# A gated linear attention and a cosine MoE layer on one core: more chunks loaded as pairs of tokens, the first ones by halves of the heads, and a new order

## The chip, the cores and the metric

The kernel runs on one core of one Trainium2 chip. The metric is the device time of one execution in microseconds (us). 13 runs of the kernel before gave a median of 196.63 us, from 194.6 to 198.44.

## What is computed

```python
# q, k, v, f_logit: (4, 8, 768, 48) float32
f = 1.0 / (1.0 + np.exp(-f_logit))
for t in range(S):
    state = f[:, :, t, :, None] * state + np.einsum('bhd,bhe->bhde', k[:, :, t], v[:, :, t])
    y[:, :, t] = np.einsum('bhd,bhde->bhe', q[:, :, t], state)
x = y.transpose(0, 2, 1, 3).reshape(3072, 384)
h = x @ w_in            # (3072, 2048)
g = h * np.cos(h)
out = g @ w_out         # (3072, 384)
```

## The kernel before

**Attention in chunks.** The 768 steps of each of the four batches are cut into six chunks of 128, 24 chunks in all, numbered 0 to 23. `decay` treats two neighbouring chunks at once: it loads f, takes exp and ln on ACT (ScalarE), sums the logarithms along the chunk with matmuls (`cum`, into PSUM), and makes the two factors `b` and `bi` with two more exps (`eb`, `ei`). `attend` then works on one chunk. It scales q and k (`qk`, on POOL), casts v (`vb`, `vz`), turns q and k so that the head dimension lies on the partitions (`tr` on PE and a copy `qkt`, or one DMA transpose `tq` for the chunks in `TURN_QK`), makes the scores (`sc`) and masks them (`am`, on DVE), makes the chunk's own share of the state (`ps`) and moves the state on (`st`, `sz`), and makes the result (`y`) directly in the transposed form that the MoE layer reads (`xe` copies it to `xT`).

**Pairs of tokens.** Chunks whose number is in `DUAL` are handled by `attend2`, two chunks at once. There a partition holds two neighbouring tokens, so that a row of a load is 384 bytes long, where that of a single chunk has 192. One load brings 384 KB for both chunks. The matmuls then work on tiles of 64 x 64 and 64 x 128, and the result is not transposed: `finish` casts it (`yb`), turns it on PE (`trx`) and copies it to `xT`. Before, `DUAL` is [0, 2, 4].

**The MoE layer.** `moe` takes units of 128, 128 and then 256 tokens. For each tile of 1024 columns in PSUM there are the w_in matmuls (`h`), a cosine on ACT (`cos`, the sine table with a shift of half pi) and a product on DVE (`g`, into `gT`). The w_out matmuls (`o`) sum 16 parts for each 128 tokens, in four pieces of four; the sum is copied (`ot`) and stored. The eight weight loads go through the `gT` buffers and are cast to bf16 (`wc`).

**What sets the order.** All operations are first collected in a `Plan` with their readers and writers. `Plan.run` (line 157) is a list scheduler: each operation has a cost for each engine that may do it, and a priority from the table `PR`; among those that can start within `WINDOW` of the earliest, the one of the lowest priority is put next on its engine. `PIN` fixes the engine for single operations. The result is a fixed order of instructions for each of the five engines. The costs only shape this order; the chip runs it as its data comes. All loads, stores and DMA transposes are issued by SP, in one queue. ACT needs two function tables, one for exp and ln and one for the sine; `gate` names for each group of four chunks the cosine that must come before its exps. There are six groups, and ten table loads. In the trace nearly all instructions carry line 257, which is the helper that records them; they are told apart by their tiles.

The SP queue of before begins with f, k, q (chunks 0 and 1), f (2 and 3), the first w_in, v (0, 1), k and q (2, 3), the second w_in, v (2, 3), k (4, 5) and the two remaining w_in. DMAs use eight semaphores in turn, so that each waits for the one eight places before it.

Of the kernel before, what the change touches and what calls it, by code (L numbers as in the profile page):

```python
# [111 lines left out]
class Op:  # L112
    __slots__ = ("seq", "eng", "fn", "prio", "table", "deps", "vals", "alloc", "start", "end",
                 "lat", "waiting", "after", "grp", "dma", "name", "prior", "cost", "made")


class Plan:
# [3 lines left out]
    PE_LAT = 180.0  # L121
    TABLE = 1290.0
    WINDOW = 30.0
# [4 lines left out]
    def op(self, name, eng, fn, reads=(), writes=(), prio=0.0, table=None, lat=0.0, grp=None,  # L128
           dma=None):
        o = Op()  # L130
# [3 lines left out]
        o.lat, o.grp, o.dma, o.prior = lat, grp, dma, []  # L134
# [22 lines left out]
    def run(self):  # L157
        free = {"PE": 0.0, "ACT": 800.0, "DVE": 3500.0, "POOL": 4500.0, "SP": 750.0}
        table, lock, bus, hot, pe_end = None, None, 0.0, 0.0, 0.0
# [9 lines left out]
        while len(order) < n:  # L169
            cand = []  # L170
            for o in ready:
# [18 lines left out]
                for e, cost in o.eng.items():  # L190
                    if e == "ACT" and lock is not None and o.grp != lock and o.table is not None:
                        continue
                    s = max(at, free[e] + (self.TABLE if e == "ACT" and o.table not in (None, table) else 0.0))
                    if pick is None or s + cost < pick[0]:
                        pick = (s + cost, s, e, cost)
# [19 lines left out]
            if e == "PE":  # L215
                hot *= math.exp((pe_end - s) / 2500.0)
                if hot < 0.5:
                    cost *= 1.9
                hot = 1.0 - (1.0 - hot) * math.exp(-cost / 2500.0)
                pe_end = s + cost  # L220
            o.start = s
            free[e] = s + cost
            if o.dma is not None:
                bus = max(s + cost + 700.0, bus) + o.dma
                o.end = bus + 1250.0
            else:
                o.end = s + cost + (self.PE_LAT if e == "PE" else 55.0 if e in ("ACT", "DVE") else 0.0)
                o.lat = o.end - s - cost
# [16 lines left out]


class Recorder:


    def __init__(self, engine, to):  # L250
        self._engine, self._to = engine, to

    def __getattr__(self, name):
        f = getattr(self._engine, name)

        def call(*a, **k):
            r = f(*a, **k)  # L257
            self._to.append(r.ins)
            return r
        return call  # L260


class Recorded:


    def __init__(self, nc):
        self.made = []
        for e in ("tensor", "vector", "scalar", "gpsimd", "sync"):
            setattr(self, e, Recorder(getattr(nc, e), self.made))


def apart(tc, o, base):
# [13 lines left out]
    if banks and len(others) == len(banks):  # L286
        for b in banks:
# [6 lines left out]
DUAL = [0, 2, 4]  # L294
FREE_GROUPS = 1
TURN_QK = range(12, 23)
PR = {
    "at": [-1.49, -6.93, -0.99, 13.27, -7.67, 4, 10, 9.5, -13.37, -12.55, -11.45, -9.46, -5.68, -7.15, -2,
          22.25, 10.19, 29.34, 19.9, 34.5, 43, 12.41, -1.95, 31.38],
    "dec": [-16.49, -13.88, -91.65, -10.62, -83.82, -35.17],  # L300
    "f": [-9.6, 0.04, -7, 14.37, 5.77, 13.7, 13.23, 18.93, 28.46, 33.49, 42.79, 22.57, 32.28, 13.8, 48.59,
          29.13, 41.13, 37.7, 30.11, 39.36, 49.42, 43.32, 46.86, 29.8],
    "h": [11.93, 4.6, -12.58, 7.32, -8.64, -9.43, 45, 2.23, 18.23, 18.63, 15.73, 4.41, 40.33],
    "k": [-7.62, -12.49, 0.44, 4.43, 2.7, -4.14, 7.69, 8.97, 12.29, 13.88, 14.32, 13.45, 12.51, 16.1, 9.18,
          19.51, 19.9, 19.74, 16.52, 18.13, 30.05, 34.16, 29.67, 47.94],
    "o": [14.78, 2.53, 13.63, 59.13, 65.36, 91.49, 25.09, 54.02, 36.97, 50.99, 62.96, 92.68, 123.05],
    "tq": [-17.43, -2.03, 6.77, 12.87, 14.04, 0.67, 25.22, 16.03, 47.81, 44.2, 43.57, 57.2, 54.62, 18.84,
          32.62, 19.95, 19.22, 16.34, 30.78, 4.33, 28.86, 63.13, 50.35, 20.78],
    "v": [-1.12, 8.51, 2.65, 15.87, 8.53, -6.56, 7.91, 9.09, 9.69, 12.52, 8.72, 6.57, 17.65, 13.3, 20.76,
          15.97, 19.8, 22.21, 13, 24.77, 21.05, 40.77, 28.44, 22.56],  # L310
    "w_in": [-3.97, 0.54, 2.78, 2.77],
    "w_out": [14.63, 52.89, 69.53, 73.7],
    "wc": [20.5, -34.04, -32.41, -65.79, -1.36, -30.8, -15, -24.5],
    "gate": [None, 8, 12, 14, 12, 32],
}
PIN = {1: "ACT", 9: "DVE", 11: "POOL", 13: "DVE", 28: "POOL", 29: "POOL", 32: "ACT", 46: "DVE", 48: "ACT", 51:
       "ACT", 64: "ACT", 92: "POOL", 93: "POOL", 94: "DVE", 96: "ACT", 111: "DVE", 113: "ACT", 116: "DVE", 158:
       "POOL", 161: "ACT", 173: "ACT", 176: "ACT", 178: "DVE", 220: "POOL", 223: "ACT", 237: "ACT", 239: "DVE",
       247: "ACT", 268: "DVE", 274: "ACT", 289: "POOL", 290: "POOL", 307: "ACT", 309: "ACT", 338: "DVE", 359:
       "ACT", 360: "POOL", 370: "ACT", 376: "POOL", 377: "ACT", 404: "ACT", 410: "DVE", 425: "ACT", 426: "POOL",  # L320
       434: "DVE", 440: "POOL", 441: "POOL", 450: "DVE", 471: "DVE", 477: "ACT", 492: "POOL", 508: "POOL", 509:
       "ACT", 539: "ACT", 560: "POOL", 561: "ACT", 570: "DVE", 576: "POOL", 577: "ACT", 624: "POOL", 633: "ACT",
       639: "POOL", 640: "POOL", 670: "DVE", 676: "DVE", 692: "ACT", 701: "DVE", 707: "POOL", 708: "ACT", 738:
       "DVE", 759: "ACT", 775: "ACT", 776: "ACT", 778: "DVE", 782: "ACT", 803: "ACT", 809: "ACT"}


def build(nc, cpool, ppool, q, k, v, f_logit, moe_w_in, moe_w_out, out, rec=None):
# [85 lines left out]
    P, nc = Plan(), rec or nc  # L413
# [17 lines left out]
    def load_weights(part, i, prio):  # L431
# [12 lines left out]
        P.op(f"w{part}{i}", {"SP": 420.0}, fn, writes=[stage], prio=prio, dma=2080.0)  # L444
# [7 lines left out]
    def load(t, src, b, c, n, prio, nm, eng="SP"):  # L452

        def fn(e):
            i_, o = (nc.scalar if e == "ACT" else nc.sync), t.ap
            if n not in DUAL:
                i_.dma_start(out=HB(o), in_=src[b, :, c * C:(c + 1) * C, :].rearrange("h p d -> p h d"))
            else:
                i_.dma_start(out=o.rearrange("p (h x) -> p h x", h=H),
                             in_=src[b, :, c * C:(c + 2) * C, :].rearrange("h (p e) d -> p h (e d)", e=2))  # L460
        P.op(nm + str(n), {eng: 430.0 if n not in DUAL else 500.0}, fn, writes=[t], prio=prio,
             dma=1000.0 if n not in DUAL else 1430.0)

# [11 lines left out]
    def decay(chunks, g, prio):  # L475
# [3 lines left out]
        pc = Val(scS if m == 2 else p1S)  # L479
        flat = lambda a: a.rearrange("p m h d -> p (m h d)")  # L480
        for i, (b, c, n) in enumerate(chunks[:1] if dual else chunks):
            load(ft.part((lambda a: flat(a)) if dual else (lambda a, i=i: a[:, i].rearrange("p h d -> p (h d)"))),
                 f_logit, b, c, n, PR["f"][n], "f")

        first = P.op("exp", {"ACT": act(384 * m, "S")}, lambda e: nc.scalar.activation(
            out=flat(ft.ap[:, 0:m]), in_=flat(ft.ap[:, 0:m]), func=AF.Exp, scale=-1.0),
            reads=[ft], writes=[ft], prio=prio, table="E", grp=g)
        gates.append((first, g))
        firsts.setdefault(g, []).append(first)
        loads = [w for p in ft.parts for w in p.writers]  # L490
# [3 lines left out]

        def ln(e):
            o, i_ = sp.ap[:, 0:m, :, 0:D], ft.ap[:, 0:m]
            if dual:
                o = o.rearrange("p e h d -> p h e d")
                i_ = i_.rearrange("p m h d -> p (m h) d").rearrange("p (h e) d -> p h e d", e=2)
            nc.scalar.activation(out=o, in_=i_, func=AF.Ln, bias=1.0)  # L500
        P.op("ln", {"ACT": act(384 * m, "S")}, ln, reads=[ft], writes=[sp], prio=prio, table="E", grp=g)
        cut = (lambda i: pc.ap[:, 512 * i:512 * i + 512]) if m == 2 else (lambda i: pc.ap)
        two = lambda j, h: sp.ap[:, j, h:h + 2, :].rearrange("p h d -> p (h d)")

        for i in range(m):
            def pe(e, i=i):
                o = cut(i)
                if dual:
                    w = sp.ap[:, :, 4 * i:4 * i + 4, 0:D]
                    v = o[:, 0:HD].rearrange("p (h e d) -> p h e d", e=2, d=D)  # L510
                    nc.tensor.matmul(v, lhsT=incl, start=True, stop=False,
                                     rhs=w[:, 0, :, None, :].broadcast_to([128, NP, 2, D]))
                    nc.tensor.matmul(v[:, :, 0, :], lhsT=strict, rhs=w[:, 1], start=False, stop=False)
                    nc.tensor.matmul(v[:, :, 1, :], lhsT=incl, rhs=w[:, 1], start=False, stop=False)
                    for p in range(2):
                        for x in range(2):
                            nc.tensor.matmul(o[:, HD + p:HD + NP:2], lhsT=two(x, 4 * i + 2 * p), rhs=half,
# [383 lines left out]
```

## Time and profile before

| | |
|---|---|
| median of 13 runs | 196.63 us (194.6 to 198.44) |
| the profiled execution | 194.6 us |
| its span from the first to the last instruction | 192.8 us |
| mean granted TensorE clock | 0.982 |
| busy: PE matmul / weight load | 173.8 us (90%) / 128.2 us (67%) |
| busy: DVE / ACT / POOL | 122.9 us (64%) / 129.3 us (67%) / 75.4 us (39%) |
| DMA queue of SP | 106240 packets, 32.78 MB, 78.3% of 16 engines |
| chain that ended last, by engine | PE 55%, DMA 19%, SP's queue 7%, ACT 6%, DVE 5% |

The span is counted from the first to the last instruction; 1.8 us of the profiled execution's time lie around it. A row of the timeline gives the start in us from the beginning of the span, the duration in us, the engine, the operation, the tile written and the tiles read with their shapes, how often in a row, and in brackets how long the engine had been idle before and what ended that. PE's matmuls overlap, so a block's cost is read from its start to the start of the next block, not from its duration. A matmul row such as `48*128` gives the part of the array in use, and then the shape of the operands. In the row of slices each digit is the busy share of 1/40 of the span in tenths; PEclk is the granted clock.

### The profile page before, as it was taken

What the parts mean: (1) busy time and instruction counts of PE and PEld (TensorE: products, weight loads), DVE (VectorE), ACT (ScalarE), POOL (GpSimd) and SP (SyncE); (2) the same over time, 40 slices, a digit from 0 to 9 for tenths busy, and PEclk for the clock granted to TensorE, in tenths of its full rate; (3) what the DMA queues carried; (4) which work ended last, traced back from release to release, by engine and by line L of the source; (5) the groups of instructions that cost most, each with busy time, mean ns of one, the idle gap of its engine ahead of it and who ended that gap; (6) DMA issues with size and microseconds to landing.
All of it is one profiled execution on the core that took longest, in us unless ns stands there. A gap on an engine that the chain in (4) does not pass through costs nothing.

```text
span 192.8 us, 5285 instructions
## 1 busy us (share of the span) xinstructions
PE 173.8 (90%) x2194; PEld 128.2 (67%) x2194; DVE 122.9 (64%) x152; ACT 129.3 (67%) x163; POOL 75.4 (39%) x119
## 2 busy tenths in 40 slices
PE   0385799999999998799999999999999999999992
PEld 0264699866688855567775668876667767787661
DVE  5147779947887571568697368895388576578200
ACT  3694768987868599595869966788866552476010
POOL 8337322309931215939761696212960420000000
PEclk9999589999999999999999999999999999999999
DMA  6999999999899888999999999999232301100222
GB/s 153 295 281 316 359 247 320 177 253 306 166 180 198 187 191 204 200 213 179 211 177 210 137 238 190 220 154 250 87 81 57 86 14 41 44 0 15 77 75 82
DMA packets 106264, 33.11 MB, mean 172 GB/s; under 512 B 99584, under 2 KB 104704, under 8 KB 106240
## 3 DMA queue, kind: packets, MB, share of 16 engines
q1 hardware_dynamic: 106240, 32.78, 78.3%
q8 instruction: 17, 0.28, 0.6%
q14 instruction: 7, 0.06, 0.1%
HBM read 25.17 MB, written 4.72 MB: 155 GB/s over the span
## 4 chain that ended last, share of the span: by engine, by line
PE 55%; DMA 19%; SPq 7%; ACT 6%; DVE 5%; issue 4%; POOL 3%; ACTq 0%; DVEq 0%; POOLq 0%
PE ps L257 55%; DMA ld<-in_v_dram 9%; SPq L257 7%; DMA gT<-in_moe_w_out_dram 4%; DMA qkt<-qk 3%; ACT cosh L257 3%; POOL qk L257 2%; DMA ld<-in_q_dram 2%; DMA f<-in_f_logit_dram 2%; DVE am L257 2%; ACT f L257 1%; DVE w_out_bf L257 1%; ACT L865 1%; DVE gT L257 1%; ACT xT L257 0%
## 5 line engine op out<-in xcount | busy, mean ns | idle before, releaser
L257 DVE TENSOR_TENSOR gT<-ps,cosh 128x1024 bf16<-128x1024 f32 x48 | 58.0, 1220 | 18.3 <-ACT cosh L257 16.3
L257 PE MATMUL ps<-xT,w_in_bf 128*128 128x256 bf16 (+1 forms) x624 | 68.5, 267 | 0.7 <-ACT xT L257 0.4
L257 PE MATMUL ps<-w_out_bf,gT 128*128 128x384 bf16 x384 | 68.3, 326 | 0.4 <-DVE w_out_bf L257 0.4
L257 ACT ACTIVATE cosh<-ps,halfpi 128x1024 bf16<-128x1024 f32 x48 | 53.0, 1113 | 23.2 <-PE ps L257 22.9
L257 PEld LDWEIGHTS <-w_in_bf 128*128 128x128 bf16 x624 | 57.2, 99 | 8.9 <-DVE xT L257 0.5
L257 PEld LDWEIGHTS <-gT 128*128 128x128 bf16 x384 | 35.3, 98 | 22.9 <-issue 0.5
L257 POOL TENSOR_TENSOR qk<-ld,b 128x384 bf16<-128x384 f32 x22 | 23.3, 1067 | 22.3 <-ACT b L257 9.7
L257 POOL TENSOR_TENSOR sz<-st,b 64x192 bf16<-64x192 f32 x32 | 16.1, 502 | 24.7 <-DVE st L257 23.1
L257 DVE TENSOR_TENSOR am<-ps,umask 128x1024 bf16<-128x1024 f32 x18 | 21.9, 1219 | 5.2 <-PE ps L257 5.1
L257 POOL TENSOR_TENSOR qk<-ld,bi 128x384 bf16<-128x384 f32 x22 | 22.6, 1037 | 0.2
L257 POOL CAST vb<-ld 128x384 bf16<-128x384 f32 x13 | 6.6, 505 | 28.8 <-DMA ld<-in_v_dram 22.3
L257 PEld LDWEIGHTS <-qk 128*128 128x128 bf16 (+1 forms) x212 | 12.5, 107 | 6.6 <-issue 2.4
L257 ACT COPY ot<-ps 128x384 f32<-128x384 f32 x14 | 6.7, 489 | 13.8 <-PE ps L257 13.7
L257 PE MATMUL ps<-ident,qk 128*128 128x128 bf16 x104 | 9.4, 240 | 4.0 <-DVE qk L257 2.2
L257 ACT ACTIVATE f<-f 128x768 f32<-128x768 f32 x12 | 9.7, 840 | 4.9 <-DMA f<-in_f_logit_dram 4.9
L257 ACT ACTIVATE b<-ps 128x776 f32<-128x776 f32 x12 | 9.9, 823 | 3.7 <-PE ps L257 2.7
L257 DVE TENSOR_TENSOR st<-ps,sz 128x384 f32<-128x384 f32 x16 | 8.8, 551 | 5.4 <-PE ps L257 4.1
L257 PEld LDWEIGHTS <-qkt 48*128 48x128 bf16 (+2 forms) x260 | 7.2, 107 | 6.8 <-issue 2.6
L257 PE MATMUL ps<-qkt 48*128 48x128 bf16 (+1 forms) x240 | 9.9, 234 | 1.8 <-ACT qkt L257 1.6
L257 DVE COPY ot<-ps 128x384 f32<-128x384 f32 x10 | 5.5, 554 | 8.7 <-PE ps L257 4.7
L257 ACT ACTIVATE bi<-ps 128x768 f32<-128x768 f32 x12 | 9.8, 818 | 0.0
L257 PE MATMUL ps<-sp,incl 128*128 128x384 bf16 (+1 forms) x12 | 4.0, 379 | 6.3 <-ACT sp L257 6.3
(64 smaller groups left out, 158.0 us busy)
## 6 DMA issues: line engine op xcount, KB each, us to landing
f<-in_f_logit_dram SPq DMA_DIRECT2D x18, 192.0 KB, 3.9
ld<-in_v_dram SPq DMA_DIRECT2D x18, 192.0 KB, 4.8
ld<-in_k_dram SPq DMA_DIRECT2D x18, 192.0 KB, 3.9
ld<-in_q_dram SPq DMA_DIRECT2D x18, 192.0 KB, 4.0
out_dram<-ot SPq DMA_DIRECT2D x18, 192.0 KB, 1.9
gT<-in_moe_w_in_dram SPq DMA_DIRECT2D x4, 768.0 KB, 7.5
gT<-in_moe_w_out_dram SPq DMA_DIRECT2D x4, 768.0 KB, 7.4
f<-in_f_logit_dram SPq DMA_DIRECT2D x3, 384.0 KB, 6.0
```

Source lines behind the costliest of these rows:

```text
L257: r = f(*a, **k)
L865: nc.scalar.preload_act_table_set("natural_log_exp_and_others")
```

## The change

- **Pairs.** `DUAL` becomes [0, 2, 4, 6, 8, 10, 12]: chunks 0 to 13, fourteen in all, are loaded and computed as pairs of tokens, where it was 0 to 5.
- **Halves.** For the pairs in `HALVED`, [0, 2], which are the first four chunks, f, k and q are each loaded by two DMAs of four heads. `decay` there runs exp, ln, cum, eb and ei once for each half of the heads, each depending only on its half, and `attend2` multiplies each half when its parts are there. v is not halved.
- **Turns.** `TURN_QK` becomes 16 to 22: q and k of chunks 12 to 15, which a DMA had turned, are turned on PE.
- **The last store.** The w_out matmuls of the last 128 tokens are made and stored in two pieces of 256 and 128 columns.
- **The order.** The planner gets new constants, a price for changes of the matmul tile form, and a limit on the loads in flight; `PR` and `PIN` have new values throughout (left out below). The engines' orders differ from beginning to end. The SP queue now begins with f by halves for chunks 0 and 2, then k, q, k, q by halves and v of chunk 0, the same of chunk 2, and then the four w_in, the first w_out, f and v of chunk 4, the second w_out, f of chunk 6, k and q of chunk 4 and the last two w_out. ACT casts no w_in any more: POOL and DVE cast two each. Of the w_out parts POOL casts three and DVE one.
- **Recording.** The instructions that an operation makes are collected by a callback of the builder, where a wrapper around the engines did it. The rule by which waits are set is the same.

Counted by instructions: of the multiplications `qk` DVE has 10 where it had 4, and POOL 38 where it had 44. PE has 140 matmuls more, POOL and SP have fewer instructions.

```diff
-DUAL = [0, 2, 4]
+DUAL = [0, 2, 4, 6, 8, 10, 12]
 FREE_GROUPS = 1
-TURN_QK = range(12, 23)
+HALVED = [0, 2]
+TURN_QK = range(16, 23)
...
-    "gate": [None, 8, 12, 14, 12, 32],
+    "gate": [None, 2, 5, 12, 18, 34],
...
-    PE_LAT = 180.0
+    PE_LAT = 150.0
+    FORM = 96.0
     TABLE = 1290.0
-    WINDOW = 30.0
+    WINDOW = 120.0
...
+                    if e == "PE" and o.form[0] != form:
+                        s = max(at, free[e] + self.FORM)
...
                 bus = max(s + cost + 700.0, bus) + o.dma
                 o.end = bus + 1250.0
+                sent.append(bus)
+                if len(sent) > 3:
+                    free[e] = max(free[e], sent[-4] + 900.0)
...
+    def load(t, src, b, c, n, prio, nm, flat=lambda a: a):
+
+        if n not in DUAL:
+            P.op(nm + str(n), {"SP": 430.0}, lambda e: nc.sync.dma_start(
+                out=HB(t.ap), in_=src[b, :, c * C:(c + 1) * C, :].rearrange("h p d -> p h d")),
+                writes=[t], prio=prio, dma=1050.0)
+            return
+        m = 2 if n in HALVED and nm != "v" else 1
+        for i in range(m):
+            w = H // m
+            dst = t.part(lambda a, i=i: flat(a)[:, i * HD:(i + 1) * HD]) if m == 2 else t
+            P.op(nm + str(n), {"SP": 470.0}, lambda e, i=i, w=w, dst=dst: nc.sync.dma_start(
+                out=(dst.ap if m == 2 else flat(dst.ap)).rearrange("p (h x) -> p h x", h=w), in_=src[
+                    b, w * i:w * i + w, c * C:(c + 2) * C, :].rearrange("h (p e) d -> p h (e d)", e=2)),
+                writes=[dst], prio=prio + 0.01 * i, dma=1500.0 / m)
...
+        halved = chunks[0][2] in HALVED
+        two = lambda j, h: sp.ap[:, j, h:h + 2, :].rearrange("p h d -> p (h d)")
+        for part in ([0], [1]) if halved else (list(range(m)),):
+            s, w = slice(part[0], part[-1] + 1), len(part)
+            of = lambda v, i=part[0]: v.parts[i] if halved else v
+            if halved:
+                for v in (sp, bt, bi):
+                    v.part(lambda a: a)
+            prio += 0.001 * part[0]
+            first = P.op("exp", {"ACT": act(384 * w, "S")}, lambda e, s=s: nc.scalar.activation(
+                out=flat(ft.ap[:, s]), in_=flat(ft.ap[:, s]), func=AF.Exp, scale=-1.0),
+                reads=[of(ft)], writes=[of(ft)], prio=prio, table="E", grp=g)
...
-                    reads=[src, dec], writes=[parts[j][i]], prio=prio)
+                    reads=[v.parts[i] if v.parts else v for v in (src, dec)], writes=[parts[j][i]], prio=prio)
...
+            pieces = [(0, d_model)] if r0 + C < n_tokens else [(0, 256), (256, d_model)]
+            for a, z in pieces:
+                po, half = Val(p1S), ot.part(lambda o, a=a, z=z: o[:, a:z]) if len(pieces) > 1 else ot
+                for s in range(4):
+                    def g2(e, i=i, s=s, po=po, a=a, z=z):
+                        for j in range(4 * s, 4 * s + 4):
+                            nc.tensor.matmul(po.ap[:, 0:z - a], lhsT=gT.ap[:, j, i * C:(i + 1) * C],
+                                             rhs=w_out_bf[:, j, a:z], start=(j == 0), stop=(j == KF - 1))
```

## The prediction, as it was put on record

> **What bounds the kernel now.** I read the page first (busy times and the 40 slices), then the table of waits, then the timeline of the first 48 us, and last the timeline of PE alone, from which I take a price for each block of matmuls.
>
> ```profile
> PE   0385799999999998799999999999999999999992
> ...
> PEclk9999589999999999999999999999999999999999
> DMA  6999999999899888999999999999232301100222
> ```
>
> Each character is 4.8 us. PE is nearly full from the fifth slice to the end: 173.8 us busy of a span of 192.8. What it lacks lies in the first four slices, in a dip at 72 to 95 us, and behind the last matmul. DMA is full for 28 slices (135 us), so early and middle stages can wait for loads although PE is the bound overall. PE's own waits name the places: 8.3 us for the first decay results (6.3 of it the very first), then in the timeline 0.41 us at 47.7 (a w_out cast whose DMA came at 46.0), 0.76 at 72.8, 1.19 at 81.2, 0.30, 0.18 and 0.35 up to 94.7. That is 3.2 us in the middle. The 1.19 us comes behind an exp that waited 2.31 us for an f load; the 0.76 comes behind a vz cast that waited 1.74 us for a v load, which delayed the cosines and with them the table load and the exp. The middle gaps are late loads. The end: the last matmul issues until 189.4, one copy of 0.48 us, one store, 192.8.
>
> The start is a race of loads:
>
> ```profile
> 11.11 1.47 ACT L257 CAST w_in_bf<-gT 128x1536 bf16<-128x1536 f32 x1
> ...
> 12.60 0.56 DVE L257 CAST vb<-ld 128x768 bf16<-128x768 f32 x1 [1.92 <-DMA ld<-in_v_dram]
> ...
> 17.67 1.47 ACT L257 CAST w_in_bf<-gT 128x1536 bf16<-128x1536 f32 x1 [2.76 <-DMA gT<-in_moe_w_in_dram]
> ...
> 23.44 2.47 PE L257 MATMUL ps<-xT,w_in_bf 128*128 128x128 bf16 x24
> ```
>
> These readers start when their load lands. The first exp starts at 4.56 on f. From f to the first w_in, 6.55 us, lie three pair loads and one weight load; from it to v, 1.49, one pair load; from v to the second w_in, 5.07, two pair loads and one weight. So a pair load of 384 KB costs 1.49 us of the stream and a weight load 2.09. A single-chunk load of 192 KB: in the stretch 44 to 77 us DMA is 94% busy at 202 GB/s, which makes 0.97 us. The last line is where the MoE matmuls begin; from there PE hardly stops.
>
> **The change, part by part. Extra PE work.** Four more chunk pairs (6, 8, 10, 12) go by tokens, and 12 to 15 are turned on PE. Prices are from start to start of neighbouring blocks:
>
> ```profile
> 48.43 0.51 PE L257 MATMUL ps<-vb,qk 64*128 64x96 bf16 x16
> 48.87 0.82 PE L257 MATMUL ps<-w_out_bf,gT 128*128 128x384 bf16 x4
> 49.63 0.64 PE L257 MATMUL ps<-qkt 48*64 48x128 bf16 x32
> 50.20 0.62 PE L257 MATMUL ps<-ident,qk 128*128 128x128 bf16 x8
> 50.66 0.33 PE L257 MATMUL ps<-vb,qk 128*128 128x96 bf16 x4
> ```
>
> In a pair: ps 0.44, both sc 0.57, each tr 0.46. From the same timeline cum is 0.43 twice, y 0.44 for the state part and 0.51 for the rest, the two trx 0.35. Four w_out matmuls took 0.76 where 16 of them take 2.61, so the entry into the small tiles costs about 0.1; three such entries. Sum 4.4 us, or 4.2 for the first pair of a batch (four matmuls without state left out).
>
> ```profile
> 100.96 0.40 PE L257 MATMUL ps<-qkt 48*128 48x128 bf16 x8
> 101.29 2.12 PE L257 MATMUL ps<-w_out_bf,gT 128*128 128x384 bf16 x12
> 103.34 0.35 PE L257 MATMUL ps<-qkt,sz 128*32 128x128 bf16 x12
> ...
> 103.85 2.77 PE L257 MATMUL ps<-w_out_bf,gT 128*128 128x384 bf16 x16
> ```
>
> In a single chunk: sc 0.33, y 0.51 (0.34 without state), tr 0.45 (77.78 to 78.23), ps 0.17, cum 0.26, two entries 0.2. Sum 1.92, or 1.47 when DMA turns it. Pairs 6, 8 and 10: 4.2 + 4.4 + 4.4 = 13.0 against 6 x 1.92 - 0.34 = 11.2, so +1.8. Pair 12: 4.2 against 2 x 1.47 - 0.17, so +1.4. Chunks 14 and 15: +0.9. The last w_out block cut at column 256: +0.05. Together **+4.2 us on PE**, all on the path, since PE is full where they stand.
>
> **The start.** The halved loads let exp and ln begin on half the heads; but in the order of the changed program f of chunk 2 is issued ahead of k and q of chunk 0, so qk can't use all of that. Half loads at 0.75: the first k half lands at 4.56 + 1.49 + 0.75 = 6.8, the last q half at 9.0. Three qk on POOL at 1.05 end at 10.2 (the fourth is on DVE), tr at 10.9, two qkt copies on DVE at 11.8. The second sc waits for the bank that ACT's last exp pair reads; that one has the vb cast of v (landed 10.5, 0.83) ahead of it, so 13.0. Then am 1.22 to 14.7, sz 0.7, y 1.0 to 16.5, yb twice, trx, and on DVE one am (1.22) ahead of the two xT: 19.0. In the trace y starts at 17.9 and yb stands behind a vb cast that waited for v.
>
> The w_in loads are moved behind all of pairs 0 and 2. They land later at first: eight pair loads stand ahead (seven after f), so w_in number two at 4.56 + 7 x 1.49 + 2 x 2.09 = 19.2 against 17.7 now, the last at 23.4 against 27.0 (the ACT cast). DVE casts number two in 0.96, so the first 24 MoE matmuls start at **20.3 instead of 23.4, -3.1 us**. They are cold either way (24 took 2.40 us there, 1.40 at 26.2), so the granted clock makes no difference.
>
> Here a rule speaks against the change. The Trainium skill, "DMA: Bandwidth & Descriptors", section "Rules for kernel authors", says to join small transfers into large ones; its measured table (64 KB in 0.95 us, 1 MB in 6.15) makes about 0.6 us fixed for each transfer. Six more transfers would put w_in 3.6 us later and the start would lose 0.5. The row says otherwise: loads in flight together follow each other at 1.49 and 2.09 us with no gap left for a fixed part, and a half still has the 384-byte rows. Bounds for a half load: 0.75 (half of 1.49) and 0.97 (a single load, same bytes, shorter rows). I take 0.75, the row with the same packets. The new wait that comes with it is for a DMA eight places earlier, now already at the ninth load, v; all later loads queue behind it on SP. That one landed at 3.8, long before the stream needs v, so nothing.
>
> **The middle.** 32 single loads (31.0 us of the stream) become 16 pair loads (23.8): -7.2 us of DMA. Four DMA turns go too, each between 1.0 (its 256 KB at the singles' pace would be 1.3; a bound from bytes) and 3.9 (median to landing). Between the last w_in and the last w_out stand five pair loads (7.5) and four weights (8.4), so that it lands at 39.3 against 46.0. The gaps of 0.41, 0.76 and 1.19 lose their cause: **-3.2 us** with the small ones. What comes next: in the third group ACT has exp and ln of pair 12 and of chunks 14 and 15 between its exps of pair 8 and 10 and the qkt copies; laid end to end they meet PE's order with less than 0.3 us to spare. New waits can't be seen in the trace of before: between 0 and 4 us, and I take **+1.5**, half of today's middle gaps.
>
> DVE gains some 8 us (six more qk of 0.6 to 1.1, two qkt, more xT, yb and ot copies), ACT and POOL lose 2 and 8. At 131 of 193 DVE stays hidden behind PE. In the runs of 60 w_in matmuls, where a tile takes PE 1.31 us and DVE 1.22, an am in between would show on PE at up to 1.2 us; that is within the 0 to 4.
>
> **The end.** The last copy is 128 wide: 0.30 (a 128-wide cast) for 0.48, and the store is a third: -0.3, between 0 and -0.6.
>
> **Sum.** 4.2 - 3.1 - 3.2 + 1.5 - 0.3 = -0.9 us: 193.7 against the profiled execution's 194.6. That execution was the fastest of 13; their median, 196.63, is 2.0 higher. I read the 2.0 as more waits for loads in the saturated stretch, and keep 1.5 of it, since that stretch is relieved: **195.2**.
>
> **The rivals.** A measurement of this kernel tells some 0.5% (1.0 us) from no change.
> (a) As summed, 195.2, or down to 192 where the new order has no waits at all and the relief takes the whole 2.0. For it: every middle gap follows a load. Against: +4.2 on the full engine is certain, the gains are not. Chance 0.50.
> (b) PE's extra work is only just paid for: the ACT queue of the third group makes 1.3 us more of new waits, 196.5. Chance 0.20.
> (c) Slower: the half loads cost 0.97 each. Twelve of them put w_in 2.6 us later, the first MoE matmul comes at 22.9 and the start gives 0.5; the sum is +1.7 and with the full 2.0 of waits 198.3. For it: 192 KB has only been seen at that price. Against: those had rows of half the length. It decides from 0.83 us for a half on, where -0.9 is used up. New waits of over 3 us in the middle would end at the same place. Chance 0.30.
>
> So the likeliest is a small gain: faster 0.50, same 0.20, slower 0.30. The range is 191.5 (no new waits) to 199.0 (rival c and some more waits); what is beyond is new waits at their upper end.
>
> **What would show it.** The MATMULs of w_in start near 20.3 with w_in's second cast just ahead on DVE; the PE pieces of pairs 6 to 12 at 4.4 us each; no PE wait for ACT sp over 0.5 us after 40 us; the DMA row below 9 before 130 us. I am wrong if w_in starts after 22 (half loads dear), or if PE idles over 4 us between 40 and 180.

## The result, and the profile after

| | before | after |
|---|---|---|
| median of the runs taken together | 196.7 us (48 runs, 194.6 to 198.5) | 193.7 us (11 runs, 192.31 to 194.03) |
| ratio after / before, 95% interval | | 0.984 [0.981, 0.987] |
| the profiled execution, its span | 194.6, 192.8 us | 193.14, 191.3 us |
| busy PE / DVE / ACT / POOL | 173.8 / 122.9 / 129.3 / 75.4 | 177.0 / 132.8 / 129.2 / 75.3 |
| DMA queue of SP: packets, share of 16 engines | 106240, 78.3% | 85744, 70.6% |

The changed kernel is 1.6% faster. The forecast, 195.2 us, was 0.7% faster: the right direction, with a gain of 1.4 us where 3.0 came. Between the two profiled executions the gain is 1.46 us, between the medians it is 3.0. That difference is where the forecast failed. The ratios and their intervals here and below leave out runs more than 1.5% above the fastest of their kernel, while the medians are of all runs, so that a ratio can differ by some 0.2% from the quotient of the medians.

The 40 slices of the page of after, and the row of SP's queue:

```profile
PE   0596979998999999999999999999999999999994
...
PEclk9997899999999999999999999999999999999999
DMA  5999999999969988989989499960001491100122
...
q1 hardware_dynamic: 85744, 31.73, 70.6%
```

Against before PE is busier in the second to fourth slice (digits 5, 9, 6 where it had 3, 8, 5), and its dip at 72 to 95 us is gone. DMA now has slices at 4 to 6 between its nines where it was full, and falls off two slices earlier. The start, in the timeline of after (start, duration, engine, operation, tiles, idle time before and what ended it):

```profile
18.99 1.46 POOL L434 CAST w_in_bf<-gT 128x1536 bf16<-128x1536 f32 x1 [0.82 <-DMA gT<-in_moe_w_in_dram]
...
20.71 1.51 PE L778 MATMUL ps<-xT,w_in_bf 128*128 128x128 bf16 x24
...
21.24 1.10 DVE L434 CAST w_in_bf<-gT 128x1536 bf16<-128x1536 f32 x1 [0.30 <-DMA gT<-in_moe_w_in_dram]
...
22.40 1.51 PE L778 MATMUL ps<-xT,w_in_bf 128*128 128x128 bf16 x24 [0.18 <-DVE w_in_bf L434]
```

The first w_in matmuls come at 20.71 (before: 23.44), right behind the first cast (done at 20.45) and before the second one has begun. Only the second 24 need it, and wait 0.18 us. All idle times of PE from here on, in the timeline of PE alone, are that one and these:

```profile
25.71 0.83 PE L778 MATMUL ps<-xT,w_in_bf 128*128 128x128 bf16 x12 [0.95 <-DVE gT L788]
...
44.57 0.40 PE L606 MATMUL ps<-ident,qk 128*128 128x128 bf16 x4 [0.62 <-DVE qk L587]
...
46.44 0.88 PE L619 MATMUL ps<-qkt 48*64 48x128 bf16 x32 [0.27 <-DVE qkt L462]
...
74.38 0.84 PE L606 MATMUL ps<-ident,qk 128*128 128x128 bf16 x12 [0.23 <-DVE qk L587]
...
89.08 0.51 PE L570 MATMUL ps<-ident,yb 128*128 128x128 bf16 x6 [0.40 <-ACT yb L462]
```

Together 2.65 us, where before had 3.19. The 0.18 still follows a load: the cast it waits for waited 0.30 us for its part of w_in. The other five do not: they end on DVE and on a cast of ACT that themselves wait for no load just before. In e6 below, where half of the loads of chunks 6 to 13 is left out, the same five stand, equal to 0.01 us. In before the largest gap came from a load, through ACT (ACT, then PE):

```profile
79.55 0.84 ACT L257 ACTIVATE f<-f 128x768 f32<-128x768 f32 x1 [2.31 <-DMA f<-in_f_logit_dram]
...
81.18 0.32 PE L257 MATMUL ps<-sp,umask 128*128 128x384 bf16 x1 [1.19 <-ACT sp L257]
```

Behind 90 us the timeline of after shows no gap of PE. The end:

```profile
187.82 0.83 PE L800 MATMUL ps<-w_out_bf,gT 128*128 128x128 bf16 x12
...
188.69 0.27 ACT L462 COPY ot<-ps 128x128 f32<-128x128 f32 x1 [0.52 <-PE ps L800]
```

The matmuls end at 188.65; 2.7 us follow (before 3.4).

So the 1.46 us divide into three: the start -2.73 (23.44 to 20.71), the body from the first w_in matmul to the end of the last matmul +1.99 (165.95 to 167.94), and the tail with the rest, -0.72.

### The profile page after: what moved, and what is told of

Read it like the earlier page. It is cut to its first block, busy times and chain, and to the rows that moved or that the text cites. A ratio compares the mean times of both kernels' runs of the same rounds, so it can differ in the third digit from the quotient of the medians.

```text
span 191.3 us, 5533 instructions
## 1 busy us (share of the span) xinstructions
PE 177.0 (93%) x2334; PEld 133.6 (70%) x2334; DVE 132.8 (69%) x166; ACT 129.2 (68%) x166; POOL 75.3 (39%) x111
## 2 busy tenths in 40 slices
DMA packets 85768, 32.07 MB, mean 168 GB/s; under 512 B 78960, under 2 KB 84208, under 8 KB 85744
## 3 DMA queue, kind: packets, MB, share of 16 engines
q1 hardware_dynamic: 85744, 31.73, 70.6%
## 4 chain that ended last, share of the span: by engine, by line
PE 76%; SPq 6%; DVE 5%; ACT 5%; DMA 4%; issue 2%; ACTq 0%
PE ps L778 32%; PE ps L800 28%; SPq L448 5%; DMA gT<-in_moe_w_in_dram 4%; PE ps L754 2%; DVE qk L587 2%; PE ps L606 2%; PE ps L716 2%; PE ps L619 2%; DVE am L625 1%; PE ps L570 1%; ACT cosh L785 1%; PE ps L666 1%; PE ps L518 1%; PE ps L729 1%
## 5 line engine op out<-in xcount | busy, mean ns | idle before, releaser
L800 PE MATMUL ps<-w_out_bf,gT 128*128 128x384 bf16 (+2 forms) x400 | 67.9, 320 | 0.0
L551 POOL TENSOR_TENSOR sz<-st,b 64x192 bf16<-64x192 f32 x32 | 17.1, 536 | 18.7 <-DVE st L544 10.1
L462 ACT COPY ot<-ps 128x384 f32<-128x384 f32 (+2 forms) x12 | 5.4, 454 | 24.9 <-PE ps L800 24.9
L625 DVE TENSOR_TENSOR am<-ps,pmask 128x1024 bf16<-128x1024 f32 x14 | 16.7, 1218 | 2.0 <-PE ps L619 1.8
L719 DVE TENSOR_TENSOR am<-ps,umask 128x1024 bf16<-128x1024 f32 x10 | 12.2, 1215 | 0.1
L526 ACT ACTIVATE b<-ps 128x776 f32<-128x776 f32 (+1 forms) x14 | 10.1, 719 | 2.7 <-DVE am L625 1.2
L486 ACT ACTIVATE f<-f 128x768 f32<-128x768 f32 (+1 forms) x14 | 10.5, 749 | 1.6 <-DMA f<-in_f_logit_dram 1.6
L587 DVE TENSOR_TENSOR qk<-ld,bi 128x384 bf16<-128x384 f32 x7 | 8.4, 1234 | 4.6 <-ACT sp L498 4.4
L498 ACT ACTIVATE sp<-f 128x768 bf16<-128x768 f32 (+1 forms) x14 | 10.5, 753 | 0.4
L462 ACT COPY qkt<-ps 128x1024 bf16<-128x1024 bf16 x7 | 7.1, 1014 | 4.7 <-PE ps L606 4.7
L526 ACT ACTIVATE bi<-ps 128x768 f32<-128x768 f32 (+1 forms) x14 | 10.1, 719 | 0.0
```

Source lines behind the costliest of these rows:

```text
L462: (nc.scalar.copy if e == "ACT" else nc.vector.tensor_copy)(out=o, in_=i_)
L486: first = P.op("exp", {"ACT": act(384 * w, "S")}, lambda e, s=s: nc.scalar.activation(out=flat(ft.ap[:, s]), in_=flat(ft.ap[:, s]), func=A ...
L526: nc.scalar.activation(out=out_.ap[:, s, :], in_=pc.ap.rearrange("p (m n) -> p m n", m=w)[:, :, 0:n], func=AF.Exp, scale=sign)
L551: eng().tensor_mul(out=like(S_out.ap, pv())[s, ..., r, :], in0=srcap()[s, ..., r, :], in1=d[..., None].broadcast_to(list(d.shape) + [D]))
L587: P.op("qk", {"POOL": 1150.0, "DVE": 800.0}, lambda e, j=j, i=i, src=src, dec=dec: E(e).tensor_mul(out=parts[j][i].ap.rearrange("p e h d - ...
L625: P.op("am", {"DVE": dve(1024)}, lambda e, sc=sc, am=am: nc.vector.tensor_mul(out=am.ap.rearrange("p r a n -> p (r a n)").rearrange("p (a ...
```

## The experiments

Three theories were open. **A**: single loads in the full stretch made before slow, and unevenly so from run to run; the 384-byte rows took that away, and this is the gain. **B**: the earlier start, made by the halved loads, is the gain. **C**: the new order is the gain, and the loads had little to do with it. Runs that stand in one group were made beside each other on one chip, with the same runs of before; each group had another chip, so kernels are compared within a group, and a comparison across groups is called one.

### First group (before: 194.28 us, 192.85 to 197.61, 43 runs)

**e1_pairs_as_two.** The changed kernel, but each load of pairs 6 to 12 is two DMAs, one for each token of the two, so that rows have 192 bytes again. Nothing else moves.

```diff
-            P.op(nm + str(n), {"SP": 470.0}, lambda e, i=i, w=w, dst=dst: nc.sync.dma_start(
...
+                    for x in range(2):
+                        nc.sync.dma_start(
+                            out=flat(dst.ap).rearrange("p (h e d) -> p e h d", h=H, e=2)[:, x],
+                            in_=src[b, :, c * C:(c + 2) * C, :].rearrange("h (p e) d -> e p h d", e=2)[x])
```

> The changed kernel, with each load of the pairs 6 to 12 made as two DMAs with 192-byte rows (one for each token of a partition); all other instructions and their orders are the same. It puts 16 x (2 x 0.97 - 1.49) = 7.2 us back on the stream of loads. Theory 1 (late loads in the saturated stretch made the middle gaps of the kernel before and the 2 us between its profiled run and its median): 1.5 to 3 us slower than the changed kernel (ratio to the kernel before 0.992 to 1.0), with PE gaps behind loads between 40 and 100 us and runs that differ by more than 2 us. Theory 2 (the gain is the start and the new order; loads had slack): at most 0.5 us slower, ratio 0.984 to 0.987.

Measured: 199.13 us (6 runs), ratio 1.027 [1.022, 1.033]. With short rows the changed kernel is slower than before. Against e3 and e4 of the same group (193.04 and 193.10), which keep the long rows, it loses 6 us, twice what was expected at most. Two lines of its timeline (of the slowest of the six, 200.21) show the place, first DVE, then PE:

```profile
61.12 0.56 DVE L434 CAST vb<-ld 128x768 bf16<-128x768 f32 x1 [5.68 <-DMA ld<-in_v_dram]
...
62.86 4.42 PE L785 MATMUL ps<-xT,w_in_bf 128*128 128x256 bf16 x20 [4.25 <-DVE gT L795]
```

A `vb` cast stands at the head of DVE's queue and waits 5.68 us for v. Behind it stand the `g` products; without them no PSUM tile comes free, and PE stands for 4.25 us. Then the matmuls start slowly: the first 20 take 4.42 us, where 12 took 1.47 just before. The granted clock is 0.50 from 62 to 68 us, and the page of the same run has two slices at 6 there:

```profile
PEclk9997999999996699999999999999999999999999
```

**e2_before_light.** The kernel before, with f, k, q and v of chunks 6 to 13 loaded for four of the eight heads; the other four heads of these chunks are computed from old data.

```diff
+                z = 4 if 6 <= n < 14 else H
-                i_.dma_start(out=HB(o), in_=src[b, :, c * C:(c + 1) * C, :].rearrange("h p d -> p h d"))
+                i_.dma_start(out=HB(o)[:, 0:z], in_=src[b, 0:z, c * C:(c + 1) * C, :].rearrange("h p d -> p h d"))
```

> The kernel before, with the loads of f, k, q and v of chunks 6 to 13 cut to four of the eight heads (the other heads keep what the buffers held); all else the same. It takes some 12 to 15 us off the stream of loads and leaves PE's work as it is. Theory 1: the middle gaps (3.2 us) and the spread go: 2 to 4 us faster than the kernel before (ratio 0.98 to 0.99), runs within 2 us of each other. Theory 2: within 0.7 us of the kernel before, with the same spread.

Measured: 190.31 us (189.97 to 190.99), ratio 0.983 [0.979, 0.987]. The order is that of before to the last instruction, and the middle gaps are gone; of the waits of PE behind 24 us one is left, the w_out cast:

```profile
47.95 0.81 PE L257 MATMUL ps<-w_out_bf,gT 128*128 128x384 bf16 x4 [0.41 <-DVE w_out_bf L257]
```

The six runs also lie within 1.0 us of each other, where the 43 of before spread over 4.8 (of six drawn from these 43 at random, 2% lie so close). That speaks for A and against C: the middle gaps of before are its loads in the full stretch, and with them lightened the old order is no slower than the new one (192.45 us in e6 below, in another group). No slow execution of before was profiled; that its spread has the same cause rests on e2's.

**e3_whole_loads.** The changed kernel, with f, k and q of the first two pairs in one DMA each; the computation still goes by halves.

```diff
-            P.op(nm + str(n), {"SP": 470.0}, lambda e, i=i, w=w, dst=dst: nc.sync.dma_start(
...
+            P.op(nm + str(n), {"SP": 470.0}, lambda e, i=i: i == 0 and nc.sync.dma_start(
+                out=flat(t.ap).rearrange("p (h x) -> p h x", h=H), in_=src[
+                    b, :, c * C:(c + 2) * C, :].rearrange("h (p e) d -> p h (e d)", e=2)),
```

> The changed kernel, with f, k and q of the first four chunks loaded whole (6 DMAs where there were 12), exp, ln, cum and qk still by halves in the same order. Theory of the prediction (a half load costs 0.75 us, halving only brings the first work forward): the first exp starts 0.7 to 0.9 us later, the first y about 0.5 to 1.0 later, w_in at the same time; 0.3 to 1.0 us slower than the changed kernel. Rival (a half load costs about 0.9 to 1.0, as the landings in the profile suggest): w_in lands 1.5 to 2 us earlier, and the time is the same within 0.3 us or shorter.

Measured: 193.04 us, ratio 0.994 [0.992, 0.996]. The first `cum` comes at 5.59 (after: 4.74), as expected, but the first w_in matmuls at 20.50. The comparison with the changed kernel itself is in the third group.

**e4_one_last_store.** The last 128 tokens in one w_out piece and one store.

```diff
-            pieces = [(0, d_model)] if r0 + C < n_tokens else [(0, 256), (256, d_model)]
+            pieces = [(0, d_model)]
```

> The changed kernel, with the last 128 tokens' w_out sum in one piece, one copy and one store. The prediction's term says 0.3 us slower than the changed kernel; the two profiles (2.6 us behind the last matmul where there were 3.4) say 0.7 to 0.8 us, less 0.05 of PE.

Measured: 193.10 us, ratio 0.996 [0.994, 0.998]; also in the third group again.

### Second group (before: 195.01 us, 192.98 to 198.7, 55 runs)

**e5_after_again.** The changed kernel as it is.

> The changed kernel as it is, on the chip of this call, so that its variants have their own base. Theory 1 (the kernel before loses by late loads, which depend on how fast a chip's loads are): its time stays at 193 to 194 us wherever it runs, and the ratio moves with the kernel before: about 0.994 where that takes 194.3, about 0.984 where it takes 196.7. Rival (the ratio is a property of the two programs): 0.984 within 0.003 again.

Measured: 192.45 us (192.04 to 193.87), ratio 0.991 [0.988, 0.994]. That interval and the first one, 0.984 [0.981, 0.987], do not meet. Over four sets of runs before has medians of 194.28, 195.01, 196.7 and 197.78, the changed kernel over three 192.45, 193.3 and 193.7. The medians of before lie 3.5 us apart, those of the changed kernel 1.25. So the ratio moves mainly with before, though the changed kernel came out below the 193 to 194 us that were expected here.

**e6_after_light.** The changed kernel with the loads of pairs 6 to 12 for four heads; the other four of these chunks are computed from old data.

```diff
+            z = w if n < 6 else 4
...
-                out=(dst.ap if m == 2 else flat(dst.ap)).rearrange("p (h x) -> p h x", h=w), in_=src[
-                    b, w * i:w * i + w, c * C:(c + 2) * C, :].rearrange("h (p e) d -> p h (e d)", e=2)),
+                out=(dst.ap if m == 2 else flat(dst.ap)).rearrange("p (h x) -> p h x", h=w)[:, 0:z], in_=src[
+                    b, w * i:w * i + z, c * C:(c + 2) * C, :].rearrange("h (p e) d -> p h (e d)", e=2)),
```

> The changed kernel, with the 16 pair loads of chunks 6 to 13 cut to four of the eight heads; all else the same. The counterpart of the cut in the kernel before, so that both are compared with loads out of the way. Theory 1: the loads already have slack here, within 0.7 us of the changed kernel, while the kernel before gained 4; then the kernel before with light loads (190.3) is the faster by about 2, which is PE's extra work less the gain of the start. Rival (the changed kernel still waits for loads too): 1.5 us faster or more.

Measured: 192.45 us, the same as e5. Halving these loads again gains nothing: no wait for a load that costs time is left in the middle.

**e7_dma_turn_14_15** and **e8_dma_turn_14_15_23.** Chunks 14 and 15 (in e8 chunk 23 as well) turned by a DMA transpose, at the place where the order has the PE turn. In e8 the turn of chunk 23 comes before chunk 20 has last read the buffer, so that the state's share of chunk 20's result is made with chunk 23's q.

```diff
+                if n in BY_DMA:
+                    nc.sync.dma_start_transpose(out=qkt.ap, in_=qk.ap)
+                    return
...
+BY_DMA = [14, 15]
```

> The changed kernel, with q and k of chunks 14 and 15 turned by DMA again, issued where the PE transposes stood; 16 PE transposes and two copies less. The price of that part of the change by itself: PE is the bound, so 0.9 us faster (0.46 for each), if DMA has room at 80 to 100 us; two more DMA turns there, where DMA is 90% busy, may push loads back: then between 0 and 1 us slower.

> As the run before it, and chunk 23 turned by DMA too, at about 155 us where DMA is nearly idle; 8 PE transposes less. 0.4 us faster than the run before it, unless its 4 us turn comes too late for the last scores: then 0 to 2 us slower.

Measured: 193.22 us, ratio 0.994 [0.991, 0.997], and 193.93, ratio 0.997 [0.994, 0.999], where e5 had 192.45. Taking 0.97 us of turns off the full engine did not help. PE in the timeline of the unchanged kernel (the run e10 below) around them:

```profile
94.89 0.50 PE L570 MATMUL ps<-ident,yb 128*128 128x128 bf16 x6
95.23 0.61 PE L703 MATMUL ps<-ident,qk 128*128 128x128 bf16 x8
95.67 0.33 PE L729 MATMUL ps<-vb,qk 128*128 128x96 bf16 x4
95.85 0.61 PE L703 MATMUL ps<-ident,qk 128*128 128x128 bf16 x8
96.38 5.45 PE L778 MATMUL ps<-xT,w_in_bf 128*128 128x256 bf16 x48
```

and of e7:

```profile
94.39 0.50 PE L571 MATMUL ps<-ident,yb 128*128 128x128 bf16 x6
94.72 0.33 PE L733 MATMUL ps<-vb,qk 128*128 128x96 bf16 x4
95.87 5.45 PE L782 MATMUL ps<-xT,w_in_bf 128*128 128x256 bf16 x48 [0.81 <-DVE xT L463]
```

From `trx` to the next w_in matmuls it is 1.49 us in one and 1.48 in the other. The matmuls need `xT`, which DVE copies behind `g`; the two turns fill just that wait. The medians are 0.8 and 1.5 us above e5, and the profiled runs show the same: from the row of w_in matmuls near 25 us to the end the unchanged kernel takes 165.5 us (e5), e7 166.5 and e8 166.9. In e7 0.44 us of that is there by the last copy, and 0.4 follows it (3.1 us from that copy's start to the end, where e5 has 2.7). e8 has a wait of 0.77 us for `st` at 158.8, and 3.4 us behind the start of its last copy. Behind 26 us PE waits for no load in either. Why the last store ends later, and what makes e7's 0.44, stays open.

### Third group (before: 197.78 us, 196.02 to 198.74, 11 runs; 6 runs of each kernel)

**e9_pairs_by_heads.** Each load of pairs 6 to 12 is two DMAs as in e1, but by heads: four heads each, with rows of 384 bytes.

```diff
+                for x in range(1 if n < 6 else 2):
+                    z = w if n < 6 else 4
...
+                        in_=src[b, w * i + 4 * x:w * i + 4 * x + z, c * C:(c + 2) * C, :].rearrange(
+                            "h (p e) d -> p h (e d)", e=2))
```

> Each load of the pairs 6 to 12 is two DMAs of four heads, 192 KB each, with rows that stay at 384 bytes; the number of DMAs is that of the run in which the same loads were split by token (rows of 192 bytes, 2.7% slower than before). Theory, the stream time of short rows is what cost there: the stream grows by no more than 0.5 us in all, so within 1 us of the changed kernel, no PE wait for gT or sz above 1 us after 50 us. Middle: a half load costs 0.89 as at the start, 16 x 0.29 = 4.6 us more of stream, one late v load, some 1 to 3 us slower. Rival, the number of DMAs on the one queue is what cost: about 5 us slower than the changed kernel, with a PE wait of about 4 us near 60 us.

**e10_after_same_chip**, **e11_whole_loads_again**, **e12_one_store_again.** The changed kernel, and the kernels of e3 and e4, side by side.

> The changed kernel unchanged, for a direct comparison with the three others of this call. A ratio to before between 0.984 and 0.991, and a median of 192.4 to 193.7 us.

> As before, f, k and q of the first two pairs loaded whole, the computation still by halves. Theory, the halving of the loads is worth little in the end: within 0.6 us of the changed kernel in this call. Rival, the start sets the end one to one: the first exp comes 0.85 us later, so 0.8 to 1 us slower than the changed kernel.

> The last 128 tokens in one w_out piece and one store. Theory: 0.7 us slower than the changed kernel in this call, all of it behind the last matmul. Rival: the change of the end is worth nothing, within 0.2 us.

| run | median (range) | ratio to before |
|---|---|---|
| e9, 16 DMAs more, long rows | 192.81 (191.97 to 193.99) | 0.977 [0.971, 0.982] |
| e10, the changed kernel | 193.30 (191.84 to 194.17) | 0.979 [0.972, 0.985] |
| e11, whole loads | 193.26 (192.68 to 193.39) | 0.979 [0.974, 0.984] |
| e12, one last store | 193.12 (192.68 to 194.44) | 0.980 [0.974, 0.985] |

e9 settles what was dear in e1: the number of DMAs is the same, the time is that of the changed kernel, and the same `vb` cast goes through without a wait in its timeline of DVE:

```profile
55.63 0.55 DVE L466 COPY ot<-ps 128x384 f32<-128x384 f32 x1
56.09 0.68 DVE L434 CAST vb<-ld 128x768 bf16<-128x768 f32 x1
56.85 1.23 DVE L792 TENSOR_TENSOR gT<-ps,cosh 128x1024 bf16<-128x1024 f32 x1
```

It is the row length, and with it the number of packets on the queue: 102384 in e1, 86000 in e9, 85744 in after. (The 0.89 us for a half load in the expectation of e9 was a misreading; the half load below has the right one.) e11 speaks against B as far as the halves go: they make the first results 0.85 to 1.0 us earlier, and the end is where it was; six runs that spread over 2 us would not show a difference of some tenths. For the last store the medians tell nothing. The traces do: in e10 2.7 us follow the start of the last copy, in e12 3.3, and the second piece costs PE 0.14 (162.95 against 162.81 from the row at 25 us to that copy). So it is worth some 0.5 us, which six such runs cannot show.

**Where the remaining spread sits.** The row of 12 w_in matmuls behind the wait of 0.94 to 0.95 us for `g` (25.71 in after) is a mark: up to it PE runs the same matmuls in the same order in after, e1, e4 to e10 and e12, yet it lies anywhere from 24.55 (e8) to 26.70 (e9). From it to the end of the span the changed kernel's three profiled runs take 165.6, 165.5 and 165.6 us, e6 165.6, e9 165.5. So in these executions the spread arises at the start, and behind 25 us the kernel is as good as fixed. PE's pace has the larger part in it: in these ten runs the first block of `y` starts at 15.86 to 16.67, and from there to the mark PE takes between 8.2 us (e7, e8) and 10.1 (e4). The `sc` block near 17.3 us takes 0.64 us in some runs and 0.42 in others. Windows of 2 us of PE in after (busy, matmuls, granted clock, DMA share, GB/s):

```profile
16.00:18.00 2.00, 1.54 (x55) 0.80 0.99 359
18.00:20.00 2.00, 2.00 (x30) 0.50 1.04 368
20.00:22.00 2.00, 2.00 (x45) 0.85 1.02 382
```

and the same of e7, where the block is fast:

```profile
16.00:18.00 2.00, 1.40 (x57) 1.00 1.04 349
18.00:20.00 2.00, 1.71 (x47) 1.00 1.00 360
```

In the window from 18 to 20 us PE starts 30 matmuls in after and is always busy; in e7 it starts 47 and has time left (partly other matmuls, since e7 is ahead by then; the `sc` block is the same in both). The Trainium skill, "TensorE: Matmul & The Clock Gate", section "Part 1: The HAM clock gate", says that the array runs at half pace until it has been busy for a window, and that the windows run freely, so that the same kernel meets them differently from run to run. That fits these rows.

**What the runs say of the theories.** A holds: without the long rows (e1) the changed kernel is the slower one, and with light loads before loses its gaps and its spread (e2). The four DMA turns that left the stretch too were not tested as a whole; e7 puts two back, and no wait for a load comes of it. B holds in part: the start of after is 2.73 us earlier and pays for most of the PE work, but not through the halves (e11). Which part of the new order it owes this to, the sequence of the loads, the casts of w_in that left ACT, or the orders of the engines, no run separates. C falls with e1, which has the new order and is slower than before, and with e2. No kernel here beats the changed one by more than the runs can tell.

## Why the prediction was too small

Step by step, between the two profiled executions:

| term | predicted | measured |
|---|---|---|
| start | -3.1 | -2.73 |
| PE's extra work | +4.2 | about +3.8 |
| pace of the first 48 w_in matmuls, and one `sc` that now lies ahead of them | 0 | about -1.3 |
| middle gaps gone, new waits | -3.2 + 1.5 | -0.54 |
| end | -0.3 | -0.72 |
| sum | -0.9 | -1.5 |
| kept of the 2.0 us between median and profiled run | 1.5 | 0.56 |

(The fourth row is 3.19 us against 2.65. The first 48 w_in matmuls took 2.40 + 1.40 us before and 1.51 + 1.35 after, without the wait; one `sc` is 0.35. The PE work is what is left of the body's +1.99.)

- **The step that failed is the last one**: "I read the 2.0 as more waits for loads in the saturated stretch, and keep 1.5 of it". The reading of the 2.0 fits e2 (spread 1.0 us instead of 4.8 with lighter loads); the conclusion from it was wrong. If the 2.0 are late loads, and the change takes the waits for loads away in that stretch, nearly all of it has to go with them. Of the 1.5 us of such waits that were kept, the runs show none: with these loads halved (e6) the median stays at 192.45 us, and behind 25 us the profiled executions of the changed kernel all take 165.5 to 165.6. What was left between its median and its profiled run is 0.56 us, and as far as the profiled runs show it comes from the start. So 0.94 of the 1.5 us that the forecast was short come from this term, and the other 0.6 from the sum above it.
- **How far it was off is partly luck.** The profiled run of before was the fastest of 48, that of after is 0.83 us above its fastest (192.31). From the fastest to the median it is 1.39 us in after, close to the 1.5, but for another reason: the 1.5 were waits for loads, the 1.39 are the spread of the start, to which the forecast gave nothing. And in the second group, where before runs better, the same two kernels gave 0.991, where the forecast makes 0.993.
- **The loads in the middle**: right, and shown by e1 and e9. The -7.2 us of stream from longer rows is what carries the gain: put back, it costs more than the whole change brings.
- **The half load** was taken at 0.75 us, and it came at that. In after, v of chunk 0 and then the last q half of chunk 2 land here, with four halves from one to the other, 3.05 us or 0.76 each:

```profile
11.33 0.83 ACT L434 CAST vb<-ld 128x768 bf16<-128x768 f32 x1 [1.36 <-DMA ld<-in_v_dram]
...
14.38 0.99 POOL L587 TENSOR_TENSOR qk<-ld,b 128x384 bf16<-128x384 f32 x1 [0.21 <-DMA ld<-in_q_dram]
```

From the first exp (3.61) to that `vb` cast the mean of the seven halves is 0.89, but this hides one pause: by the landing times in the trace the third half of f comes 2.06 us after the second (1.2 to 1.9 in the other runs with these halves). So the 0.97 us of rival (c) did not come. The second w_in part was late all the same, at 21.24 where 19.2 was forecast: the first two w_in loads took 5.7 us behind v of chunk 2 (15.50 to 21.21), where 2 x 2.09 was put, and with whole loads (e11) still 5.3. Why the pause and why these two are slower stays open. By the forecast's own path (21.24 and a cast of 1.10) the matmuls would have started at 22.3 and the start given 1.1 us. It was kept by a second error in the other direction: the forecast let the first 24 matmuls wait for the second w_in part, and they need only the first. That 20.71 lies near the forecast's 20.3 is two errors that cancelled, not a right step.
- **The rule** on small transfers that was set against the change is not borne out in the full stretch. The some 0.6 us fixed for each are an estimate from the table of the Trainium skill, "DMA: Bandwidth & Descriptors", section "Bandwidth", which was measured on transfers that GpSimd issues, where SP issues them here. By it e9's 16 additional DMAs would cost 9.6 us of stream, more than the 7.2 that e1 put back, and e9 lost nothing.
- **The granted clock** was said to make no difference. It made about 0.9 us of difference in these two executions: the first 24 w_in matmuls took 2.40 us before and 1.51 after. PE in before, where they begin (the granted clock is 0.50, where after has 0.85 and 1.00 around its own):

```profile
22.00:24.00 2.00, 2.00 (x30) 0.50 1.04 374
```

It differs from run to run, so it belongs into the range and not into the sum.
- **PE's extra work** came out at the prices of the rows (`tr` 0.46, `y` 0.43 and 0.51, `ps` 0.47, `cum` 0.43 in after). The sum has a slip: for pairs 6 to 10 it takes off 0.34 for chunks without state, where only chunk 6 has none, 0.17; put right it is 4.0. That the turns of chunks 14 and 15 are "all on the path" was wrong: with their 0.97 us taken out (e7), a wait of 0.81 us for `xT` stands in their place, and the next matmuls start 0.01 us nearer.
- **New waits** were taken at 1.5 us; behind 40 us it is 1.52 (0.62, 0.27, 0.23, 0.40). The 1.13 us at 22 to 26 were not foreseen: 0.18 for the second w_in cast, and 0.95 until a `g` is done.
- **The end** was put at -0.3, between 0 and -0.6. The copy gives 0.21 (0.48 to 0.27), and the rest of the 0.72 is the store behind it; with the split's price on PE, e10 and e12 make it 0.5.

Of the three cases (a) came, between its sum and the 192 us that it gave as its lower end. What stays true of (b) is that the PE work is dear: with light loads in both, the old order takes 190.31 us (e2) and the new one 192.45 (e6, another group), although the new one starts earlier.

## What to carry to other kernels

Before adding a profiled execution's gain to a median, ask what makes the runs differ: if it is what the change removes, the gap between the median and that execution belongs to the gain, and a kernel with its loads lightened measures it. Look also where the profiled execution stands among its runs, before and after. An operation on a full engine is on the path only where the next one is ready; taking it off may leave the same wait bare. When loads fill the queue, as here, try longer rows before fewer loads, and look at which loads stand at the head of the queue of an engine on which the main chain depends.

## What was not expected of the hardware

- Rows of 192 instead of 384 bytes, with the same bytes and the same number of DMAs, made the kernel 6 us slower (199.13 in e1, against 193.04 and 193.10 for e3 and e4 of the same group, and 192.81 for e9 in another). Sixteen more DMAs alone cost nothing measurable.
- A PE wait of 4.25 us cost more than itself: 20 matmuls behind it took 4.42 us, 0.22 each, where 0.12 each was the pace before it.
- With the granted clock recorded at 1.00 the same block took 0.42 us in e7 and 0.64 in e4 (near 17.3 us in both): the record does not always show the slow pace, the durations do.
- With no load that holds PE for more than 0.2 us behind 20 us, the profiled runs of one order still differ by 2.15 us in their first 25 (24.55 to 26.70).
